# Padding x to 128 rows, splitting the first batch's stores, and retiming two ends of a Fourier and mixture kernel on one Trainium2 core

## The chip, the cores and the metric

The kernel runs on one core of one Trainium2 chip. A core has a matrix engine (PE, whose weight loads are listed as PEld), a vector engine (DVE), a scalar engine (ACT), GpSimd (POOL), and a sync engine (SP) that here issues nearly all DMAs. The metric is device time in microseconds, the median of three runs; one further run was taken with the hardware profiler, and the trace is of that one. Lower is better.

## The reference

For each of 8 batches x is 3136 rows of 256 numbers, float32.

```python
X = np.fft.rfft(x, axis=1)                   # along the 3136 rows
Yr = Xr @ w_r - Xi @ w_i + b_r               # complex product with a 256x256 matrix
Yi = Xr @ w_i + Xi @ w_r + b_i
Y  = soft_threshold(Yr, 0.01) + 1j * soft_threshold(Yi, 0.01)
y  = np.fft.irfft(Y, n=3136, axis=1)
scores = y @ w_gate                          # per row
top = the 128 rows of each batch with the highest scores
out = y;  out[top] += sigmoid(scores[top]) * (relu(y[top] @ w1) @ w2)
```

## The kernel before

3136 is 98 x 32, so the transform is done in two stages. **Stage one** (`s1`) transforms along the 98 rows of a unit, which is one quarter of a pair's columns: a batch has U = 8 units, and two neighbouring units share one load of x (`ld_x`) and one store (`store` inside `s1`). The tile for x has 128 partitions, of which 98 (partitions 15 to 112, two halves of NH = 49) hold data and the rest must be finite; partitions 0 to 14 are set to zero once at the start. A unit can be given to the matmuls as it was loaded (8 matmuls), or first be **folded**: `fold` makes the sum and the difference of the two column halves with two elementwise instructions on DVE or POOL, and then 4 matmuls do. The result goes through a copy on ACT to a tile `at` or `ot` and from there to DRAM (`As`).

**Stage two** (`s2`) reads `As` back transposed: `ld_a(b, g)` with g = 0, 4, 8 loads four groups, each from 16 of the 48 rows of each half, and `s2` transforms along the 32. `spectral` multiplies with the weights (split into two float32r parts each, made by `weights` on DVE), POOL makes the bias tile `kb`, `shrink` does the threshold, and `s2i` goes back along the 32 and writes `Cs` to DRAM. `ld_c` and `s1i` do the inverse along the 98 and store the output. The router (`score`, `select`, `place`) finds the 128 best rows by fixing their threshold digit by digit: each of the eight rounds is a short DVE chain, one small matmul (L254) and again DVE. `fetch` gathers the rows by an indirect DMA on POOL, `ffn` computes the two layers.

The order on every engine is the order in which the code is written; nothing is rescheduled. `units` is a list of T = 100 (batch, group) pairs, and step t of the main loop issues, in this order: stores that were put off (`flush`), loads for later steps, `s2` of unit t + 1, one stage-one unit or inverse unit (`pair`), `spectral` of unit t, folds on POOL, perhaps a second `pair`, and `s2i` of unit t - 1. Before the loop stands the **head**: all of batch 0's stage one, the weights, and 24 matmuls on constants (`warm`). After the loop stands the **tail**: rounds (t counts on from T) in which the last batch's router steps (`turn`), its inverse units and the two layers of the last batches (`work`) take turns; `fill` and `idle` add matmuls on constants. The last batch's gather waits for its rows to be stored, and its two layers come last.

DMAs issued by SP complete through eight semaphores used in turn, so each waits until the eighth DMA before it has landed; all DMAs of one queue share 16 DMA engines.

Of the kernel before, what the change touches and what calls it, by code (L numbers as in the profile page):

```python
# [19 lines left out]
B, S, D = 8, 3136, 256  # L20
N1, N2, NH = 98, 32, 49
# [90 lines left out]
def fourier_moe(ctx: ExitStack, tc: tile.TileContext, x, w_r, w_i, b_r, b_i, wg, w1, w2,  # L112
                t_w, t_wi, t_wq, t_g, t_gi, t_gt, t_gti, t_m, t_dig, outs, cap):
    nc = tc.nc
# [10 lines left out]
    As, Cs, xt, sd, at, ct, av, cv, ot, X, Y, Csc = [{} for _ in range(12)]  # L125
# [4 lines left out]
    def c_tile(shape, dt, name):  # L130
        return const.tile(shape, dt, name=name)
# [6 lines left out]
    xts, cvs = [whole[:, k] for k in range(2)], [c_tile([128, 8, D], F32, "cv" + str(k)) for k in range(2)]  # L138
# [20 lines left out]
    def ld(out, src):  # L159
        nc.sync.dma_start(out=out, in_=src)  # L160
# [188 lines left out]
    def prepare(b, k, idx, xe):  # L349
        n = min(128, cap - 128 * k)  # L350
        px = ps.tile([128, 2, n], F32, name="m", bufs=1)
        for h in range(2):
            nc.tensor.transpose(out=px[:, h, :], in_=xe[:, h * 128:(h + 1) * 128], identity=ident[:n, :n])
        load[0] += 0.25
        xT = pool.tile([128, 2, n], F32, name="xT", bufs=1)
        nc.vector.tensor_copy(xT, px)
        junk = pool.tile([n, D], F32, name="junk", bufs=1)
        sg = pool.tile([n, 1], F32, name="sg")
        nc.vector.tensor_tensor_reduce(out=junk, in0=xe, in1=wgb[:n], scale=1.0, scalar=0.0,
                                       op0=ALU.mult, op1=ALU.add, accum_out=sg)  # L360
        ga = pool.tile([n, 1], F32, name="ga")
        nc.scalar.activation(out=ga, in_=sg, func=AF.Sigmoid)
        return xT, ga

    def pause():
        t = done["t"]
        while done["t"] == t:
            yield

    def hidden(b, k, xT, hs):  # L370
        n = min(128, cap - 128 * k)
        for q in range(FF // 512):
            ph = ps.tile([128, 4, n], F32, name=bank(b, 1 + q % 2), bufs=1)
            for f in range(4):
                if f > 0:
                    yield
                for h in range(2):
                    nc.tensor.matmul(ph[:, f, :], w1s[:, h, (4 * q + f) * 128:(4 * q + f + 1) * 128], xT[:, h, :],  # L378
                                     start=(h == 0), stop=(h == 1))
                load[0] += 0.45  # L380
            hs.append(pool.tile([128, 4, n], F32, name="hh", bufs=2))
            nc.scalar.activation(out=hs[q], in_=ph, func=AF.Relu)
            if done["t"] < T:
                yield from pause()
            else:
                yield

    def combine(b, k, idx, xe, ga, hs):
        n = min(128, cap - 128 * k)
        py = ps.tile([n, D], F32, name=bank(b, 3), bufs=1)  # L390
        for f in range(FF // 128):
            if f > 0:
                yield
            nc.tensor.matmul(py, hs[f // 4][:, f % 4, :], w2s[:, f, :], start=(f == 0), stop=(f == FF // 128 - 1))  # L394
            load[0] += 0.43
        ye = pool.tile([n, D], F32, name="ye", bufs=1)
        nc.vector.scalar_tensor_tensor(out=ye, in0=py, scalar=ga, in1=xe, op0=ALU.mult, op1=ALU.add)
        nc.gpsimd.indirect_dma_start(out=outs[b], out_offset=bass.IndirectOffsetOnAxis(ap=idx, axis=0),
                                     in_=ye, in_offset=None)
        yield  # L400

    def ld_x(b, i):
        if i % 2:
            return
        k = i // 2
        t = (cvs if b < 2 and k > 1 else xts)[k % 2]
        xt[b, k] = t.rearrange("p (h c) d -> p h c d", h=2)
        ld(t[15:113].rearrange("p c d -> p (c d)"), x[b, k])

    def fold(b, i, eng):  # L410
        e = i % 2
        t = xt[b, i // 2][:, :, 2 * e:2 * e + 2, :]
        f = sd[b, i] = pool.tile([128, 2, 2, D], F32, name="sd", bufs=2)
        for k, op in enumerate((ALU.add, ALU.subtract)):
            eng.tensor_tensor(out=f[:113, k], in0=t[:113, 0], in1=t[:113, 1], op=op)  # L415

    def s1(b, i, first=None):
        e = i % 2
        if (e == 0 if first is None else first):
            if b not in As:  # L420
                As[b] = dram.tile([2, NH, N2, D], F32, name="As")
            at[b] = pool.tile([128, 2, 2, 2 * D], F32, name="ot" if b == 0 and i > 3 else "at", bufs=2)
        p = ps.tile([128, 2, 2 * D], F32, name="px" if b == 0 and e else "s", bufs=1)
        if (b, i) in sd:
            f = sd.pop((b, i))
            parts = [[(c, f[:, c])] for c in range(2)]
        else:
            f = [xt[b, i // 2][:, h, 2 * e:2 * e + 2, :] for h in range(2)]
            parts = [[(c, f[0]), (2 * c, f[1])] for c in range(2)]
        for k in range(len(parts[0])):  # L430
            for r in range(2):
                for c in range(2):
                    v, f = parts[c][k]
                    nc.tensor.matmul(p[64 * c:64 * c + 64, r, :], w[64 * r:64 + NH * r, v, :], f[64 * r:64 + NH * r],  # L434
                                     start=(k == 0), stop=(k == len(parts[0]) - 1))
        t = at[b]
        nc.scalar.copy(out=t[:, :, e, :], in_=p)  # L437
        if (e == 0 if first is None else first):
            return
        i = i | 1  # L440

        def store():
            nc.sync.dma_start(out=As[b].rearrange("q m n d -> (q m) n d")[:, 4 * i - 4:4 * i + 4, :], in_=t[15:113])
        stores.append(store)

    def ld_a(b, g):
# [190 lines left out]
    def fill(us):  # L637
        idle(max(0, round((us - load[0]) / 0.216)))
        load[0] = 0.0

    def idle(n):
        if n == 0:
            return
        p = ps.tile([128, 2, 2 * D], F32, name="s", bufs=1)
        for i in range(n):
            nc.tensor.matmul(p[:, 0], wts[0][0][:, 0, :128], wts[0][0].rearrange("p h d -> p (h d)"), start=True, stop=True)

    YB, XB, KB, RB, AB = 2, 2, 1, 1, 2
    G, U = 13, 8
    units = [u for b in range(0, B, 2) for u in [(b, g) for g in range(G)] + [(b + 1, g) for g in range(G - 1)]]  # L650
    units.insert(13, units.pop(12))
    T = len(units)
    LEAD, LAG = 17, 18
    stores, spreads = [], []
    done = {"s2i": -1, "s1i": -1, "t": -1, "c7": 1000, "rep": -1}
    thrs, slots = {}, {}

# [31 lines left out]
    def ffn():  # L689
        for e in range(B * NCHK):  # L690
            while not fetched or done["t"] < age[fetched[0][:2]] or done["t"] < T - 2 and fetched[0][0] > B - 4:
                yield
            item = fetched[0]
            if item[0] == B - 1:
                idle(12)
            xT, ga = prepare(*item)
            if item[0] < B - 1:
                yield from pause()
            else:
                yield  # L700
            hs = []
            yield from hidden(*item[:2], xT, hs)
            yield from combine(*item, ga, hs)
            fetched.pop(0)
# [30 lines left out]
    def flush():  # L735
        for f in stores:
            f()
        del stores[:]
# [4 lines left out]
    for i in range(U):  # L743
        ld_x(0, i)
    warm(8)
    for k, t in enumerate(xts + cvs):
        (nc.gpsimd if k % 2 else nc.vector).memset(t[:15], 0.0)
    consts_a()
    consts_g(0)
    consts_c()  # L750
    for i in range(0, U, 2):
        fold(0, i, nc.vector)
        s1(0, i + 1, True)
        s1(0, i, False)
        flush()
        if i == 4:
            ld_x(1, 0)
    weights()
    warm(24)
    ld_a(0, 0)  # L760
    ld_x(1, 2)
    ld_x(1, 4)
    ld_x(1, 6)
    first = {i - 1: i for i in range(U)}
    fold(1, 0, nc.gpsimd)
    fold(1, 1, nc.gpsimd)
    rest = [(b, i) for b in range(B) for i in range(U)]
    for t in range(-1, T):
# [50 lines left out]
        if 0 <= t - 1 < T:  # L819
            b, g = units[t - 1]  # L820
# [5 lines left out]
    t = T  # L826

    def ready():
        b, i = rest[0]
        return b < B - 1 or t > T + 2  # L830

    def work(us, alone=False):
        turns = 0
# [11 lines left out]
    while threads or ffns:  # L845
        done["t"] = t
        flush()
        load[0] = 0.0
        if t == T:
            work(0.8, True)  # L850
            fill(1.6)
            s2i(*units[T - 1])
            done["s2i"] = B - 1
            flush()
            load[0] = 0.0
            work(0.8, True)
            ld_last(0, 2, True)
            ld_last(2, 1, True)
            ld_last(3, 1, False)
        load[0] = 0.0  # L860
        turn("pe", "da", "db")
        us = 0.4 if t == T else 1.2 if t < T + 11 else 0.6
        work(us, t < T + 2)
        if threads:
            fill(min(us, 1.0))
        t += 1


# [27 lines left out]
```

## Time and profile before

| | us |
|---|---|
| median of 3 runs (lowest, highest) | 698.48 (697.32, 702.02) |
| profiled execution, its own time | 692.63 |
| its span, first to last instruction | 690.4 |

The engines were busy for these shares of the span: PE 94%, PEld 70%, DVE 63%, ACT 53%, POOL 42%. The mean granted PE clock was 0.976 of full. In the chain that ended last PE has 65%, DVE 14%, DMA 7%. A share is a mean over stages with different limits, so the head and the tail are to be read by their own rows.

### The profile page before, as it was taken

The numbers are of one execution on the slowest core, as the hardware profiler recorded it, in microseconds if no ns is written. First come the engines' busy times: TensorE is split into PE (matmuls) and PEld (weight loads), VectorE is DVE, ScalarE is ACT, GpSimd is POOL, SyncE is SP. The second block draws the span as 40 slices with busy tenths as digits, with TensorE's granted clock in tenths as the row PEclk, the third lists the DMA queues.
The fourth block names the chain that finished last, engine by engine and source line by source line (L and its number), as shares of the span: only waits on it lengthen the run. The fifth ranks groups of instructions, "written<-read, shape, count | busy, mean of one in ns | idle before, by whom it ended". The sixth has DMA issues, their size and how long they took to land.

```text
span 690.4 us, 20349 instructions
## 1 busy us (share of the span) xinstructions
PE 650.7 (94%) x8391; PEld 481.8 (70%) x8391; DVE 434.5 (63%) x1384; ACT 364.5 (53%) x672; POOL 287.7 (42%) x243
## 2 busy tenths in 40 slices
PE   7689989999999999999999999999999999998896
PEld 3457767767777777777777777677777777676465
DVE  5326565677687766766677655776587667775531
ACT  3236465566655567655645555655655545554230
POOL 3247555555555555355445443554452222221001
PEclk9889999999999999999999999999999999999779
DMA  8799857798989898979578668879867636978540
GB/s 247 283 261 330 264 168 215 226 303 269 287 258 311 285 304 248 339 222 292 181 213 292 218 226 269 254 251 278 240 207 232 193 117 192 291 230 275 156 149 23
DMA packets 72748, 165.64 MB, mean 240 GB/s; under 512 B 4624, under 2 KB 58354, under 8 KB 60146
## 3 DMA queue, kind: packets, MB, share of 16 engines
q1 hardware_dynamic: 71472, 162.00, 74.7%
q0 software_dynamic: 896, 2.17, 1.1%
q8 instruction: 66, 1.08, 0.7%
q10 hardware_dynamic: 288, 0.18, 0.1%
q14 instruction: 26, 0.21, 0.1%
HBM read 85.23 MB, written 79.17 MB: 238 GB/s over the span
## 4 chain that ended last, share of the span: by engine, by line
PE 65%; DVE 14%; DMA 7%; ACT 5%; issue 5%; POOL 2%; SPq 1%; POOLq 0%; ACTq 0%; DVEq 0%
PE pca L531 10%; PE s L614 6%; DVE junk L543 5%; PE py L233 5%; PE px L470 5%; PE py L234 5%; PE py L235 5%; PE s L434 5%; PE pcb L233 4%; PE m L378 3%; PE m L394 3%; PE pcb L235 2%; PE pcb L234 2%; DVE Xl L483 2%; ACT ct L541 2%
## 5 line engine op out<-in xcount | busy, mean ns | idle before, releaser
L499 POOL TENSOR_TENSOR kb<-ks,bias 128x512 f32<-128x512 f32 x100 | 128.0, 1280 | 308.2 <-ACT ks L497 307.0
L415 POOL TENSOR_TENSOR sd<-xt 113x512 f32<-113x512 f32 x104 | 130.5, 1277 | 31.7 <-DMA xt<-in_x 23.7
L503 DVE TENSOR_TENSOR py<-py,kb 128x512 f32<-128x512 f32 x100 | 70.0, 700 | 80.5 <-POOL kb L499 75.9
L541 ACT COPY ct<-pcb 128x256 f32<-128x256 f32 (+1 forms) x100 | 37.2, 372 | 151.3 <-PE pcb L531 135.0
L531 PE MATMUL pca<-Y,gi_sb 64*64 64x256 f32 x760 | 101.8, 386 | 5.4 <-DVE pca L251 4.8
L483 DVE TENSOR_TENSOR Xl<-px,Xh 128x768 fp32r<-128x768 f32 x100 | 95.7, 957 | 17.6 <-ACT Xh L482 17.4
L531 PE MATMUL pcb<-Y,gi_sb 64*64 64x256 f32 x768 | 103.0, 386 | 0.0
L543 DVE CUSTOM_DVE_ANT_0 junk<-pcb,wgb 128x256 f32<-128x256 f32 (+1 forms) x100 | 42.4, 424 | 88.2 <-ACT ct L541 87.3
L470 PEld LDWEIGHTS px<-g_sb,av 64*64 64x64 f32 x3072 | 78.1, 134 | 16.6 <-issue 2.7
L482 ACT CAST Xh<-px 128x768 fp32r<-128x768 f32 x100 | 81.1, 811 | 14.8 <-PE px L470 13.4
L470 PE MATMUL px<-g_sb,av 64*64 64x96 f32 x3072 | 83.3, 244 | 3.3 <-issue 2.3
L616 ACT COPY ot<-s 128x1024 f32<-128x1024 f32 x58 | 60.1, 1036 | 43.0 <-PE s L614 43.0
L531 PEld LDWEIGHTS pca<-Y,gi_sb 64*64 64x64 f32 x760 | 46.4, 132 | 40.9 <-DVE pca L251 11.5
L508 ACT ACTIVATE r<-py,m2l 128x512 f32<-128x512 f32 x100 | 70.5, 705 | 6.7 <-DVE py L503 6.7
L510 DVE SCALAR_TENSOR_TENSOR Y<-py,r 128x512 f32<-128x512 f32 x100 | 68.5, 685 | 1.6 <-ACT r L508 1.6
L233 PE MATMUL pcb<-wsh,Xh 128*128 128x256 f32 x200 | 65.6, 328 | 1.5 <-DVE Csc L543 1.5
L434 PE MATMUL s<-sd,w 64*64 64x512 f32 x480 | 65.0, 600 | 0.8 <-ACT ot L616 0.8
L614 PE MATMUL s<-cv,wi_sb 64*64 64x512 f32 x464 | 63.0, 612 | 0.0
L437 ACT COPY at<-s 128x1024 f32<-128x1024 f32 x58 | 60.6, 1045 | 3.0 <-PE s L434 2.9
L233 PE MATMUL py<-wnh,Xh 128*128 128x256 f32 x200 | 56.9, 285 | 3.2 <-DVE Y L510 3.0
L234 PE MATMUL pcb<-wsh,Xl 128*128 128x256 f32 x200 | 56.2, 281 | 0.0
L235 PE MATMUL pcb<-wsl,Xh 128*128 128x256 f32 x200 | 56.1, 281 | 0.0
(186 smaller groups left out, 1356.6 us busy)
## 6 DMA issues: line engine op xcount, KB each, us to landing
Cs<-ct SPq DMA_DIRECT2D x48, 512.0 KB
av<-As SPq DMA_DIRECT2D x46, 512.0 KB
As<-at SPq DMA_DIRECT2D x30, 784.0 KB
cv<-Cs SPq DMA_DIRECT2D x30, 784.0 KB
out<-ot SPq DMA_DIRECT2D x30, 784.0 KB
xt<-in_x SPq DMA_DIRECT2D x28, 784.0 KB
cv<-in_x SPq DMA_DIRECT2D x4, 784.0 KB
As<-ot SPq DMA_DIRECT2D x2, 784.0 KB
```

What stands on the lines that cost most here:

```text
L233: nc.tensor.matmul(out, wh, mh, start=start, stop=False)
L234: nc.tensor.matmul(out, wl, mh, start=False, stop=False)
L235: return nc.tensor.matmul(out, wh, ml, start=False, stop=stop).ins
L415: eng.tensor_tensor(out=f[:113, k], in0=t[:113, 0], in1=t[:113, 1], op=op)
L434: nc.tensor.matmul(p[64 * c:64 * c + 64, r, :], w[64 * r:64 + NH * r, v, :], f[64 * r:64 + NH * r], start=(k == 0), stop=(k == len(parts[0 ...
L470: nc.tensor.matmul(o[:, :, N2 * j:N2 * j + N2], a[64 * p:64 * p + 64, j, g % 4, 128 * h + 64 * q:128 * h + 64 * q + 64], g_sb[64 * p:64 * ...
L482: nc.scalar.copy(out=vh, in_=v)
L483: nc.vector.tensor_tensor(out=vl, in0=v, in1=vh.bitcast(F32), op=ALU.subtract)
L499: nc.gpsimd.tensor_tensor(out=kb[:r], in0=ks[:r].broadcast_to([r, 2, D]), in1=bias[:r], op=ALU.add)
L531: nc.tensor.matmul(p[q][64 * a:64 * a + 64], gi_sb[64 * q:64 * q + 64, g, c, 64 * a:64 * a + 64], y[64 * q:64 * q + 64, c, :], start=(c == ...
L543: nc.vector.tensor_tensor_reduce(out=junk[:r], in0=p[k][:r], in1=wgb[:r], scale=1.0, scalar=0.0, op0=ALU.mult, op1=ALU.add, accum_out=Csc[ ...
L614: nc.tensor.matmul(p[64 * c:64 * c + 64, r, :], wi_sb[64 * r:64 + NH * r, b // (B - 1), 15 * c:15 * c + 64], f[64 * r:64 + NH * r, 4 * c + ...
```

## The change

- x is padded on the host with 15 zero rows ahead and 15 behind, and `ld_x` fills all 128 partitions; the four memsets of the first 15 partitions go.
- For batch 0 a pair's store is issued in parts: the first 16 rows of each half at once, the other 32 rows of each half and the two last rows (`others`) later: for the first two pairs after the next pair's or the one behind it, for the last two behind `ld_a(0, 0)`.
- In the head units 4 to 7 are all folded (six units of eight instead of four), on DVE.
- The loads of batch 1's x are all issued behind those stores, the first of them ahead of `ld_a(0, 0)`; batch 1's stage-one units run one step later in the loop (`first`), and so do their folds.
- In the tail the inverse units of the last batch start one round later, a round may take up to 1.3 instead of 1.2 of the planner's units of work up to T + 3, and `idle(12)` is `idle(8)`.

```diff
-        ld(t[15:113].rearrange("p c d -> p (c d)"), x[b, k])
+        ld(t.rearrange("p c d -> p (c d)"), x[b, k])
...
+        v = As[b][:, :, 4 * i - 4:4 * i + 4, :]
+
         def store():
-            nc.sync.dma_start(out=As[b].rearrange("q m n d -> (q m) n d")[:, 4 * i - 4:4 * i + 4, :], in_=t[15:113])
+            if b > 0:
+                ld(v.rearrange("q m n d -> (q m) n d"), t[15:113])
+                return
+            for q in range(2):
+                ld(v[q, :16], t[15 + NH * q:31 + NH * q])
+            later.append(others)
+
+        def others():
+            for q in range(2):
+                ld(v[q, 16:48], t[31 + NH * q:63 + NH * q])
+            ld(v[:, 48], t[63:113:NH])
...
             if item[0] == B - 1:
-                idle(12)
+                idle(8)
...
     warm(8)
-    for k, t in enumerate(xts + cvs):
-        (nc.gpsimd if k % 2 else nc.vector).memset(t[:15], 0.0)
...
     for i in range(0, U, 2):
         fold(0, i, nc.vector)
-        s1(0, i + 1, True)
-        s1(0, i, False)
+        if i > 3:
+            fold(0, i + 1, nc.vector)
+        s1(0, i + (i < 4), True)
+        s1(0, i + (i > 3), False)
         flush()
-        if i == 4:
-            ld_x(1, 0)
+        if i in (2, 4):
+            later.pop(0)()
+    ld_x(1, 0)
     weights()
     warm(24)
     ld_a(0, 0)
-    ld_x(1, 2)
-    ld_x(1, 4)
-    ld_x(1, 6)
-    first = {i - 1: i for i in range(U)}
+    for f in later:
+        f()
+    for i in (2, 4, 6):
+        ld_x(1, i)
+    first = {i: i for i in range(U)}
...
-        return b < B - 1 or t > T + 2
+        return b < B - 1 or t > T + 3
...
-        us = 0.4 if t == T else 1.2 if t < T + 11 else 0.6
+        us = 0.4 if t == T else 1.3 if t < T + 4 else 1.2 if t < T + 11 else 0.6
         work(us, t < T + 2)
         if threads:
-            fill(min(us, 1.0))
+            fill(us if t < T + 5 else min(us, 1.0))
...
     xl = np.asarray(inputs["x"]).reshape(B, 2, NH, 4, 2, 4, D).transpose(0, 3, 4, 2, 1, 5, 6).reshape(B, 4, N1, 8 * D)
+    xl = np.pad(xl, ((0, 0), (0, 0), (15, 15), (0, 0)))
```

How this moves instructions is seen best in the order on each engine. First SP in the head, before: `in_x` is the input, `As` the scratch in DRAM, `av` what `ld_a` fills, and the size is that of the destination.

```order
L160 DMA g_sb<-t_g 128x768
L443 DMA As<-at 98x2048 x2
L443 DMA As<-ot 98x2048
L160 DMA xt<-in_x 98x2048
L443 DMA As<-ot 98x2048
L160 DMA av<-As 128x2x256 x4
L160 DMA xt<-in_x 98x2048
```

And with the change:

```order
L160 DMA As<-at 16x2048 x4
L160 DMA As<-at 32x2048 x2
L160 DMA As<-at 2x2048
L160 DMA As<-ot 16x2048 x2
L160 DMA As<-at 32x2048 x2
L160 DMA As<-at 2x2048
L160 DMA As<-ot 16x2048 x2
L160 DMA xt<-in_x 128x2048
L160 DMA av<-As 128x2x256 x4
L160 DMA As<-ot 32x2048 x2
L160 DMA As<-ot 2x2048
```

Where four stores of 98 rows stood ahead of the reads into `av`, the 16-row parts of all four pairs and the rest of the first two now do; the rest of the last two stands behind them, and the load of x stands right ahead of them instead of ahead of the last store.

Then PE at the end of the head and the start of the loop, before: L434 is `s1` (x8 unfolded, x4 folded), L633 `warm`, L470 `s2`.

```order
L434 MATMUL px<-cv_83,w 64x512 x8
L434 MATMUL s<-sd,w 64x512 x4
L434 MATMUL px<-cv_84,w 64x512 x8
L434 MATMUL s<-sd,w 64x512 x4
L633 MATMUL px<-Xh 128x512 x24
L470 MATMUL px<-g_sb,av 64x3x32 x16
L434 MATMUL s<-sd,w 64x512 x4
L470 MATMUL px<-g_sb,av 64x3x32 x16
```

And with the change, where `warm` is L645 and `s2` L482:

```order
L434 MATMUL s<-sd,w 64x512 x8
L434 MATMUL px<-sd,w 64x512 x4
L434 MATMUL s<-sd,w 64x512 x4
L434 MATMUL px<-sd,w 64x512 x4
L645 MATMUL px<-Xh 128x512 x24
L482 MATMUL px<-g_sb,av 64x3x32 x32
L434 MATMUL s<-sd,w 64x512 x4
```

Sixteen matmuls of two units became eight, and the first two `s2` stand next to each other, with no stage-one unit between them.

Last PE in the tail, before, from the second digit's matmul (L254) on: L614 is an inverse unit, L394 the second layer, L328 the end of `place` for the batch before the last.

```order
L254 MATMUL pcb<-digits,n 128x15
L328 MATMUL pca<-row,hot 128x34
L328 MATMUL pca<-neg,hot 128x34
L328 MATMUL pca<-row,hot 128x34
L328 MATMUL pca<-neg,hot 128x34
L614 MATMUL s<-xt,wi_sb 64x512 x4
L394 MATMUL py<-w2s,hh 128x256
L254 MATMUL pcb<-digits,n 128x15
L614 MATMUL px<-xt,wi_sb 64x512 x4
L394 MATMUL py<-w2s,hh 128x256
L254 MATMUL pcb<-digits,n 128x15
```

And with the change, where an inverse unit is L626:

```order
L254 MATMUL pcb<-digits,n 128x15
L328 MATMUL pca<-row,hot 128x34
L328 MATMUL pca<-neg,hot 128x34
L328 MATMUL pca<-row,hot 128x34
L328 MATMUL pca<-neg,hot 128x34
L394 MATMUL py<-w2s,hh 128x256 x4
L254 MATMUL pcb<-digits,n 128x15
L626 MATMUL s<-xt,wi_sb 64x512 x4
L626 MATMUL px<-xt,wi_sb 64x512 x4
L254 MATMUL pcb<-digits,n 128x15
```

Four second-layer matmuls now stand ahead of the third digit, the first inverse unit behind it, and then two inverse units stand between two digits where one of them and a second-layer matmul stood.

## Rows read from the trace of the kernel before

**Rows 1.** Sums by stretch: us, length, busy by engine (instructions), granted clock, DMA share, GB/s.
```profile
34.60:60.00 25.40, 22.91 (x303) 16.20 (x304) 10.46 (x20) 12.79 (x21) 14.15 (x13) 0.87 0.97 286
160.00:300.00 140.00, 137.75 (x1941) 102.87 (x1941) 100.13 (x329) 86.83 (x161) 69.85 (x57) 1.00 0.91 292
647.30:664.40 17.10, 17.10 (x68) 7.15 (x67) 8.36 (x43) 5.52 (x7) 1.01 (x1) 0.50 0.41 129
62.50:64.50 2.00, 2.00 (x16) 1.52 (x13) 1.93 (x4) 2.00 (x4) 1.00 (x1) 1.00 1.06 430
```

**Rows 2.** Instructions by time on DVE, head: start, length, what, [idle before <- what ended it].
```profile
6.93 1.29 DVE L415 TENSOR_TENSOR sd<-xt 113x512 f32<-113x512 f32 x2 [1.24 <-DMA xt<-in_x]
...
13.53 1.29 DVE L415 TENSOR_TENSOR sd<-cv 113x512 f32<-113x512 f32 x2 [1.87 <-DMA cv<-in_x]
16.49 1.29 DVE L415 TENSOR_TENSOR sd<-cv 113x512 f32<-113x512 f32 x2 [1.67 <-PE px L434]
...
22.82 0.48 DVE L628 MEMSET Y<- 128x512 f32 x1
```

**Rows 3.** Instructions by time on SP, head.
```profile
21.50 0.31 SPq L443 DMA_DIRECT2D As<-ot  x1
31.79 1.92 SPq L160 DMA_DIRECT2D av<-As  x4
```

**Rows 4.** Instructions by time on PE, end of the head and first steps.
```profile
24.01 8.27 PE L633 MATMUL px<-Xh 128*128 128x512 f32 x24 [3.66 <-ACT Xh L630]
34.61 1.24 PE L470 MATMUL px<-g_sb,av 64*64 64x96 f32 x32 [2.33 <-issue]
35.67 1.30 PE L434 MATMUL s<-sd,w 64*64 64x512 f32 x8
37.82 1.56 PE L470 MATMUL px<-g_sb,av 64*64 64x96 f32 x32 [0.85 <-DVE Xl L483]
...
44.27 0.89 PE L470 MATMUL px<-g_sb,av 64*64 64x96 f32 x32
...
48.87 0.35 PE L233 MATMUL py<-wnh,Xh 128*128 128x256 f32 x1 [1.51 <-DVE Y L510]
...
51.39 0.84 PE L470 MATMUL px<-g_sb,av 64*64 64x96 f32 x32
...
56.29 0.84 PE L470 MATMUL px<-g_sb,av 64*64 64x96 f32 x32
```

**Rows 5.** Instructions by time on POOL, first steps.
```profile
45.28 1.27 POOL L499 TENSOR_TENSOR kb<-ks,bias 128x512 f32<-128x512 f32 x1
```

**Rows 6.** Instructions by time on PE, tail.
```profile
645.39 1.09 PE L614 MATMUL s<-xt,wi_sb 64*64 64x512 f32 x8 [1.42 <-DMA xt<-Cs]
...
650.40 1.99 PE L614 MATMUL s<-xt,wi_sb 64*64 64x512 f32 x8
...
665.36 0.23 PE L294 MATMUL pca<-tm,mask 98*64 98x98 bf16 x1
...
671.09 3.70 PE L394 MATMUL py<-w2s,hh 128*128 128x256 f32 x16
674.44 3.10 PE L646 MATMUL s<-wsh 128*128 128x512 f32 x12
677.38 0.38 PE L353 MATMUL m<-ident,xe 128*128 128x128 f32 x2
```

**Rows 7.** Instructions by time on DVE, tail.
```profile
645.30 0.16 DVE L251 TENSOR_TENSOR pcb<-digits,pcb 128x1 uint32<-128x1 uint32 x1
647.28 0.17 DVE L261 TENSOR_SCALAR ok<-pcb 128x15 f32<-128x15 f32 x1 [1.81 <-PE pcb L254]
648.62 0.16 DVE L251 TENSOR_TENSOR pcb<-digits,pcb 128x1 uint32<-128x1 uint32 x1
```

**Rows 8.** The gathers (L342): the last by time, and the line's issue to landing.
```profile
673.08 0.97 POOL L342 DMA_INDIRECT xe<-out,idx  x1 [11.12 <-DMA out<-ot]
DMA to landing us min/median/max: 2.7/6.3/8.3
```

More of the change, by code (lines that the diff above doesn't have):

```diff
@@ L653, in fourier_moe @@
     LEAD, LAG = 17, 18
-    stores, spreads = [], []
+    stores, spreads, later = [], [], []
     done = {"s2i": -1, "s1i": -1, "t": -1, "c7": 1000, "rep": -1}
```

## The prediction

> **What bounds the kernel now.** I read the sums by stretch first, for the granted clock and PE's idle time, then PE, DVE and SP in order of time at both ends. In the long middle PE is the bound: in 140 us it is busy for 137.75 at full clock, beside a DMA share of 0.91 [rows 1]. Nothing the change touches can help there, so its worth lies in the head and the tail.
>
> In the head three waits follow each other. The loads of x arrive 3.3 us apart (folds that wait for them start at 6.93 and 13.53, two loads later), and the fourth fold waits for PE, not for its load [rows 2]. The last store is issued at 21.50, yet SP can issue the reads of `av` only at 31.79, when all of it has landed [rows 3]. So PE, though it fills 24.01 to 32.28 with constant matmuls, waits 2.33 us for its first `s2` at 34.61 [rows 4]. Then the clock is low: 0.87 over 25.4 us is 6.6 us at half, 1.2 instead of 2.4 GHz [rows 1]. The third `s2` is 6.45 us behind the second and the fourth 7.12 behind that, where the next needs 4.90 [rows 4]. Part of the 7.12 is a wait of 1.51 for `Y` [rows 4]: POOL made the first `kb` only at 45.28, with no idle time before it, since a fold stood ahead in its queue [rows 5].
>
> In the tail the third digit's matmul stands behind the first inverse unit, which waits 1.42 us for its data; the digit was ready at 645.30 + 0.16 [rows 6, 7]. PE, which stood still until 645.39, has half the clock from 647.3 to 664.4 although it is then busy for all 17.1 us [rows 1, 6]. An inverse unit takes 1.99 us there, against 1.09 before [rows 6].
>
> **The head, step by step.** *Loads of x.* They grow from 803 to 1049 KB. No row shows a 128-row load of x. At the old rate (803 KB in 3.3 us, 243 GB/s) one takes 4.3 us; at the 430 GB/s of the stretch in which 128-row loads of tables dominate, 2.4 us [rows 1]. I take 2.5 to 3.0, nearer the second, as it is a 128-row load too; up to 3.3 the result is the same, because folds and copies then bound the head. The Trainium skill ("DMA: Bandwidth & Descriptors", the section on why a DMA increments its semaphore by 16) speaks against this: a transfer runs on the largest number of engines up to 16 that divides its rows, so 98 rows go over 14 and 128 over 16, and each engine gets 8 rows for 7. Estimated by that page a load takes 3.3 x 8/7 = 3.8 us, and the sum below would lose 1.8 us. No row here shows the engines of a load apart. The memsets that go are worth nothing: the first fold waited for its load, not for DVE [rows 2].
>
> *Stage one.* Two more units folded are 2 x 1.29 us on DVE [rows 2] and save PE about 1 us each. A fold needs the tile of the second fold before it, and a unit the bank of the unit two before it, so a pair still takes about the 2.96 us between the last two folds [rows 2]. The last copy ends near 21.3 (before: the store at 21.50) [rows 3]. Last fold's end: 19.1 in place of 17.78. `weights` stands behind it on DVE and takes 5.5 us to 23.30 [rows 2], so `warm` starts at 24.01 + 1.4 = 25.4. Its 24 matmuls took 8.27 us [rows 4], at full clock 24 x 3.10/12 = 6.2 [rows 6]; I take 7.6 and a first `s2` at 33.0 (31.6 to 33.7).
>
> *Stores and reads.* The reads of `av` now wait for 16-row parts alone. The last part is issued near 21.7 and lands about 23.5. Then a load of x (2.4 us) is ahead of `av` on the DMA engines, and 0.5 MB of `av` serves the first `s2`: ready near 28.5, bounds 27 and 31. Either is covered by `warm` until 33.0; without that cover it would be worth another 2 to 5 us. The 20 stores in place of 4 each wait on SP for the eighth DMA before them, but 14 are issued while PE and DVE finish the head and the other 6 stand behind `av`.
>
> *First steps.* `s2` number two no longer has a stage-one unit before it: it waits the 2.15 us from 35.67 to 37.82 in which both copies of the first are made [rows 4], so it starts at 33.0 + 1.06 + 2.15 = 36.2, not 37.82: **-1.6**. From there to the third, 6.45 us at half clock become about 4.0 (4.90 without the 0.9 of `s2i`): **-2.4**. From the third to the fourth, 4.90 for 7.12, as `kb` now stands ahead of the fold on POOL: **-2.2**. The stage-one unit that moved out returns at step 7, whose data is there: **+1.0** (1.30 with some half clock in row 35.67). The wait of 2.15 us may bring the clock down again; half the chance of 1.7 us is **+0.8**. Head: **-4.4**, between -7 and +2.4 (loads at 4.3 us each).
>
> **The tail.** Four second-layer matmuls, 8 instructions of 3.70/16 us [rows 6], fill PE from the end of `place` (645.39 - 1.42 = 643.97) to 645.8; the third digit follows at once instead of behind the first inverse unit and one such matmul, and the data of that unit, for which PE waited until 645.39, has then landed. PE no longer waits 1.42 us there, and I expect the clock to stay up. A round is then two inverse units at 1.05 and a digit at 0.3, 2.4 us; the DVE part of 1.50 (647.28 to 648.78) [rows 7] fits beside them. Three rounds bring the sixth digit to 653.1, the next two (one unit each, and the transposes) the last to 657.3, and the mask's matmul comes at 658.6, not 665.36 [rows 6]: **-6.8**. From there to the last transposes it was 12.02 us. Fewer first-layer matmuls stand between `place`'s steps, and `idle(8)` saves 4 x 0.26; I count 6.9 us to the gather and its 2.7 us to landing [rows 8], 9.6: **-2.4**. The gather waited for the last output store [rows 8]; with the last unit near 656 that lands near 661 and is no bound. Tail: **-9.2**, between -10.5 and -1.5. The rest of the end, from 677.38, is the same.
>
> **Sum.** The profiled execution took 692.63 us: 692.63 - 4.4 - 9.2 = 679.0. The median of the timed runs lies 5.85 above it, which I keep: **685**.
>
> **Rivals.** *The clock falls in the tail all the same.* Two inverse units at 1.99 and a digit are then 4.4 us a round, and PE has the same work at half clock. For it: the fall at 647.3 came with PE busy again for 2 us, and while busy it stayed low for 17 us [rows 1]. Against: the idle time before it goes. Tail -2, so 698.5 - 4.4 - 2 = 692. Chance 0.18.
>
> *Loads at eight rows per engine take 3.8 us.* The fourth x lands 2 us later and the whole head chain through `weights` and `warm` shifts 1.8: 687. The page above states this; the 430 GB/s speak against it. Chance 0.10.
>
> *The head's time is given back.* If the queue (share 0.97 from 34.6 to 60 [rows 1]) holds `av` for the fifth group or the x of the first steps late, PE waits there instead: head 0, total 689. Chance 0.10.
>
> *Slower.* The queue becomes the bound of the middle. If the rate of an x load and not its rows is fixed, each takes 1.0 us longer, on engines busy 0.91 in the stretch [rows 1]; PE hardly waits for DMA there now. It decides when that share reaches 1.0. The head is then 2.4 us worse, and if half of 24 x 1.0 us shows on PE, even with the tail's gain it is 698.5 + 2.4 + 12 - 9.2 = 704, and 713 without. Chance 0.05.
>
> That the change is void in the tail (the order on PE the same) is excluded by the order shown ahead; in the head the reads could still wait for whole stores, but then `s2` comes near 34 and only about 1 us is lost.
>
> **How the numbers follow.** The forecast, with 0.57, spans 678 to 691: the median's 5.85 may shrink or stay, head and tail move within their bounds. With the rivals the range is **677 to 694**. About 1%, 7 us, is what a measurement of this kernel tells from no change, so faster begins at 691.5. Faster: most of the forecast (0.54), a third of the first rival, most of the next two: 0.75. Slower over 1%: 0.05. Within: 0.20.
>
> **What would show it.** Right: folds of x 2.5 to 3 us apart; `av` issued near 23.5; `warm` running straight into `s2` near 33; no wait for `Y` near 41; fourth `s2` near 45; granted clock 1.00 from 640 to 680, rounds of 2.4 us, the last gather near 665. Wrong: a clock of 0.50 anywhere after 640, or PE waiting for a DMA between 45 and 75. If the middle's DMA share rises past 0.95 with PE waiting for it, the slower rival holds.

## The result and the profile after

| | before | changed |
|---|---|---|
| median of 4 runs each on one chip, us | 700.25 | 678.38 |
| lowest, highest | 697.32, 702.46 | 677.42, 681.79 |
| profiled execution, its own time | 692.63 | 677.42 |
| its span, and mean granted clock | 690.4, 0.976 | 675.5, 0.995 |

The ratio is 0.9699, with a 95% interval of 0.9644 to 0.9754: faster, as forecast, and 6.6 us below the forecast of 685, inside its range. The ratios here and below leave a kernel's slow runs out, so where before has runs near 686 a ratio can stand closer to 1 than the medians do.

Between the two profiles 14.9 us of span went. Three marks on PE divide them: the first digit's matmul of the last batch (640.07, now 634.00: 6.07 won in the head), the mask's matmul (665.36, now 652.45: 6.84 more) and the last transposes (677.38, now 662.49: 1.98 more). From there to the end nothing changed.

First the sums by stretch of the changed kernel (columns as in [rows 1]), for the first steps, the middle, and the tail from the first inverse unit to the mask and on to the last transposes.

```profile
31.60:60.00 28.40, 25.32 (x369) 18.58 (x370) 13.50 (x27) 14.80 (x26) 19.10 (x16) 0.94 0.85 306
160.00:300.00 140.00, 137.38 (x1939) 102.85 (x1936) 100.18 (x328) 86.55 (x161) 72.31 (x58) 1.00 0.87 298
...
640.46:652.45 11.99, 11.78 (x92) 5.36 (x92) 7.84 (x41) 7.91 (x9) 1.01 (x1) 1.00 0.86 281
652.45:662.49 10.04, 8.92 (x54) 7.58 (x53) 2.81 (x16) 1.20 (x2) 1.97 (x2) 1.00 0.29 98
```

The middle is what it was (PE 137.38 of 140 us); its DMA share fell from 0.91 to 0.87 in spite of the padded loads. The tail has its full clock throughout, where [rows 1] has 0.50. Next DVE in the head, by time (columns as in [rows 2]).

```profile
6.40 1.29 DVE L415 TENSOR_TENSOR sd<-xt 113x512 f32<-113x512 f32 x2 [4.99 <-DMA xt<-in_x]
9.18 1.29 DVE L415 TENSOR_TENSOR sd<-xt 113x512 f32<-113x512 f32 x2 [1.48 <-DMA xt<-in_x]
11.71 1.29 DVE L415 TENSOR_TENSOR sd<-cv 113x512 f32<-113x512 f32 x2 [1.24 <-DMA cv<-in_x]
13.31 1.29 DVE L415 TENSOR_TENSOR sd<-cv 113x512 f32<-113x512 f32 x2 [0.31 <-PE s L434]
15.59 2.50 DVE L415 TENSOR_TENSOR sd<-cv 113x512 f32<-113x512 f32 x4 [0.98 <-PE s L434]
...
23.13 0.48 DVE L640 MEMSET Y<- 128x512 f32 x1
```

The folds that wait for x start at 6.40, 9.18 and 11.71, 2.65 us apart on average in place of 3.3; the folds behind them wait for PE. SP in the same stretch, by time:

```profile
21.75 1.61 SPq L160 DMA_DIRECT2D As<-ot  x2
23.47 0.36 SPq L160 DMA_DIRECT2D xt<-in_x  x1
25.40 1.92 SPq L160 DMA_DIRECT2D av<-As  x4
```

From the issue of the last two parts that `av` waits for to the issue of `av` it is now 3.65 us, where the last whole store took 10.29 [rows 3]. PE from the constant matmuls on, by time:

```profile
24.32 7.24 PE L645 MATMUL px<-Xh 128*128 128x512 f32 x24 [5.09 <-ACT Xh L642]
31.62 0.89 PE L482 MATMUL px<-g_sb,av 64*64 64x96 f32 x32
34.48 1.56 PE L482 MATMUL px<-g_sb,av 64*64 64x96 f32 x32 [1.97 <-DVE Xl L495]
35.81 1.93 PE L434 MATMUL s<-sd,w 64*64 64x512 f32 x8
...
39.99 0.89 PE L482 MATMUL px<-g_sb,av 64*64 64x96 f32 x32
...
45.14 0.43 PE L543 MATMUL pca<-Y,gi_sb 64*64 64x256 f32 x2 [0.72 <-DMA gi_sb<-t_gi]
...
46.06 0.84 PE L482 MATMUL px<-g_sb,av 64*64 64x96 f32 x32
```

`warm` runs straight into the first `s2`, 2.99 us sooner than in [rows 4]; the fourth `s2` is 5.33 sooner. Behind the wait of 1.97 us the clock is low for a short stretch (1.56 for an `s2` that takes 0.89). The wait of 1.51 for `Y` is gone, since POOL makes the first `kb` at 39.17 ahead of a fold that starts at 40.42 ([rows 5]: 45.28). A new, smaller one of 0.72 has come, for the table `gi_sb` of `s2i`. PE in the tail, by time:

```profile
639.55 0.30 PE L254 MATMUL pcb<-digits,n 128*128 128x15 f32 x2
640.46 1.09 PE L626 MATMUL s<-xt,wi_sb 64*64 64x512 f32 x8 [0.61 <-DMA xt<-Cs]
641.34 1.07 PE L626 MATMUL px<-xt,wi_sb 64*64 64x512 f32 x8
642.34 0.39 PE L254 MATMUL pcb<-digits,n 128*128 128x15 f32 x2
...
644.60 0.39 PE L254 MATMUL pcb<-digits,n 128*128 128x15 f32 x2
...
652.45 0.23 PE L294 MATMUL pca<-tm,mask 98*64 98x98 bf16 x1
...
662.49 0.41 PE L353 MATMUL m<-ident,xe 128*128 128x128 f32 x2 [1.12 <-DMA xe<-out,idx]
```

The third digit stands ahead of the first inverse unit, whose wait is 0.61 in place of 1.42 [rows 6]; inverse units stay at 1.09 us, and a round of two of them and a digit takes 2.2 to 2.3 us, where a round with a single unit took 3.3 (units of 1.99 us [rows 6]). The last gather on POOL, issued at 673.08 in [rows 8], is now issued 13.48 us sooner:

```profile
659.60 0.97 POOL L342 DMA_INDIRECT xe<-out,idx  x1 [18.08 <-PE py L394]
```

### The profile page after: what moved, and what is told of

Read it like the earlier page. It is cut to its first block, busy times and chain, and to the rows that moved or that the text cites. A ratio compares the mean times of both kernels' runs of the same rounds, so it can differ in the third digit from the quotient of the medians.

```text
span 675.5 us, 20324 instructions
## 1 busy us (share of the span) xinstructions
PE 636.5 (94%) x8371; PEld 475.3 (70%) x8371; DVE 433.4 (64%) x1386; ACT 363.5 (54%) x672; POOL 284.3 (42%) x241
## 4 chain that ended last, share of the span: by engine, by line
PE 61%; DVE 14%; DMA 7%; issue 6%; ACT 5%; POOL 4%; SPq 1%; POOLq 0%; ACTq 0%; DVEq 0%
PE pca L543 10%; PE s L626 5%; DVE junk L555 5%; PE py L233 5%; PE px L482 5%; PE py L234 4%; PE py L235 4%; PE s L434 4%; PE pcb L233 4%; PE m L378 3%; PE m L394 3%; DVE Xl L495 2%; PE pcb L235 2%; PE pcb L234 2%; POOL kb L511 2%
## 5 line engine op out<-in xcount | busy, mean ns | idle before, releaser
L482 PEld LDWEIGHTS px<-g_sb,av 64*64 64x64 f32 x3072 | 77.9, 134 | 14.2 <-DVE Xl L495 2.2
L482 PE MATMUL px<-g_sb,av 64*64 64x96 f32 x3072 | 83.0, 244 | 2.0 <-DVE Xl L495 2.0
L434 PE MATMUL s<-sd,w 64*64 64x512 f32 x480 | 64.4, 599 | 2.3 <-ACT at L437 1.2
L626 PE MATMUL s<-cv,wi_sb 64*64 64x512 f32 x464 | 61.4, 598 | 0.0
```

Source lines behind the costliest of these rows:

```text
L482: nc.tensor.matmul(o[:, :, N2 * j:N2 * j + N2], a[64 * p:64 * p + 64, j, g % 4, 128 * h + 64 * q:128 * h + 64 * q + 64], g_sb[64 * p:64 * ...
L626: nc.tensor.matmul(p[64 * c:64 * c + 64, r, :], wi_sb[64 * r:64 + NH * r, b // (B - 1), 15 * c:15 * c + 64], f[64 * r:64 + NH * r, 4 * c + ...
```

## The experiments

The experiments ran on different chips, and before's median lay between 697.16 and 700.25 beside them. A difference of 1 to 2 us between two variants of the changed kernel is therefore not told by medians alone; the profiles say which wait it is.

**The tail alone.** Before, with these lines:

```diff
-                idle(12)
+                idle(8)
...
-        return b < B - 1 or t > T + 2
+        return b < B - 1 or t > T + 3
...
-        us = 0.4 if t == T else 1.2 if t < T + 11 else 0.6
+        us = 0.4 if t == T else 1.3 if t < T + 4 else 1.2 if t < T + 11 else 0.6
...
-            fill(min(us, 1.0))
+            fill(us if t < T + 5 else min(us, 1.0))
```

> The kernel before with the tail's edits alone (inverse units one round later, rounds of 1.3, 8 instead of 12 constant matmuls); head, loads and stores as before. Theory: PE no longer waits for the first inverse unit's data, so the granted clock stays at 1.00 from 640 to 665; a round takes 2.2 to 2.4 us instead of 3.3, the mask's matmul comes 6 to 7 us earlier counted from the end of the loop, the last gather another 2 us: the profiled span falls by 8 to 10 us, ratio about 0.985. Rival: the gain of the change lies in the head and in the fewer constant matmuls, and the tail's order is worth nothing by itself: about 1 to 2 us, ratio 0.997 to 0.999, half clock from 647 on as before.

Measured: 685.02 us against 698.95, ratio 0.9836 (0.9772 to 0.9900); span 681.0, 9.4 below before's. The first digit stands at 639.92, where it was; from it to the mask 17.91 us in place of 25.29, to the last transposes 10.08 in place of 12.02, and no half clock in either stretch. So it is as the theory had it, and the rival's 1 to 2 us are out. By the medians it is more, 13.9 us; why is taken up with the prediction below.

**The head alone.** The changed kernel with those lines as they were before.

> The changed kernel with the tail's edits undone: padded loads, folds, divided stores and the later second batch stay. Theory: the head's 5 to 6 us stay (first digit near 634, as in the changed kernel), the tail takes what it took before (first digit to the last transposes 37 us, with half clock and rounds of 3.3 us): span about 684.5, ratio about 0.992. Rival: the shift by 6 us alone lets the data of the first inverse unit be there, or the clock stay up; then the tail is short too, span about 676.

Measured: 692.68 us (689.41 to 696.31) against 698.95; ratio 1.0016 (0.9961 to 1.0070); span 690.2. The tail came out as the theory said: 26.44 us from the first digit to the mask, at half clock. PE there, by time:

```profile
645.25 1.11 PE L626 MATMUL s<-xt,wi_sb 64*64 64x512 f32 x8 [2.58 <-DMA xt<-Cs]
...
647.30 0.45 PE L254 MATMUL pcb<-digits,n 128*128 128x15 f32 x2
647.67 1.99 PE L626 MATMUL px<-xt,wi_sb 64*64 64x512 f32 x8
```

Its head did not. The same code reached the first digit at 638.76, not near 634: the wait for `gi_sb` was 2.19 us here, and half clock followed it. PE at that place:

```profile
47.59 0.43 PE L543 MATMUL pca<-Y,gi_sb 64*64 64x256 f32 x2 [2.19 <-DMA gi_sb<-t_gi]
...
48.51 1.18 PE L482 MATMUL px<-g_sb,av 64*64 64x96 f32 x32
49.44 1.95 PE L434 MATMUL s<-sd,w 64*64 64x512 f32 x8
```

By this profile the head is worth 1.3 us, by the changed kernel's 6.1, by the medians 6.3; the interval of the ratio has 1 in it. That the head's edits alone make the kernel faster is therefore not shown beyond the noise.

**Constant matmuls in the wait.** Before, with one addition:

```diff
+                if rest[0] == (B - 1, 0):
+                    idle(7)
```

> The kernel before with 7 constant matmuls (about 1.5 us) put on PE directly ahead of the last batch's first inverse unit, where PE waited 1.42 us for data; the order of all other work is the old one. Theory: the granted clock falls at 647 because PE stood still there, so with the matmuls it stays at 1.00, inverse units take 1.09 instead of 1.99 us, rounds about 2.2 us, and the mask's matmul comes 5 to 8 us earlier: ratio 0.988 to 0.993. Rival: the order of digit and inverse unit is what counts, not the clock: the matmuls fill time that was empty, the clock falls as before, span the same or up to 1.5 us longer.

Measured: 688.00 us against 698.95, ratio 0.9883 (0.9814 to 0.9951). PE, by time:

```profile
647.66 1.09 PE L614 MATMUL s<-xt,wi_sb 64*64 64x512 f32 x8 [0.70 <-DMA xt<-Cs]
...
649.22 0.29 PE L254 MATMUL pcb<-digits,n 128*128 128x15 f32 x2
649.44 1.09 PE L614 MATMUL px<-xt,wi_sb 64*64 64x512 f32 x8
...
651.11 0.39 PE L254 MATMUL pcb<-digits,n 128*128 128x15 f32 x2
```

The order is before's; inverse units take 1.09 us, a round 2.0, and the mask comes 19.55 us after the first digit, 5.74 less than before. So the clock, not the order, is most of what was won ahead of the mask.

**Before, once more**, unchanged:

> The kernel before once more, unchanged, for a second profile of it: its runs lie between 685 and 701 us, while the one profiled took 692.63 and the changed kernel's lie within 677 to 682. Theory: the runs differ by how long the granted clock stays at half, in the head and from 647 on; this profile shows either a longer half clock in one of the two places or, in a run near 687, none in the tail. Rival: they differ by waits for DMAs in the middle of the kernel, with the clock the same.

Measured: 689.65 us, span 687.4. This profile is of another kind than the first: the head is 4.45 us later (first `s2` at 39.06), and the tail keeps its clock. PE, by time:

```profile
644.62 0.30 PE L254 MATMUL pcb<-digits,n 128*128 128x15 f32 x2
...
649.15 1.09 PE L614 MATMUL s<-xt,wi_sb 64*64 64x512 f32 x8 [0.62 <-DMA xt<-Cs]
...
650.70 0.29 PE L254 MATMUL pcb<-digits,n 128*128 128x15 f32 x2
...
662.38 0.23 PE L294 MATMUL pca<-tm,mask 98*64 98x98 bf16 x1
```

The unchanged code needs 17.76 us here from the first digit to the mask: 7.53 less than in its other profile; what differs on PE ahead of the fall is the wait for the first inverse unit, 0.62 for 1.42. The profiles so far line up on that: after waits of 1.42 and 2.58 the clock fell, after 0.61, 0.62 and 0.70 it did not. The length of the wait alone is no rule, though. The third try below waited 1.22 there and kept its clock, and in the head of before a longer wait than the tail's, the 1.51 for `Y` [rows 4], was followed by full clock (columns as in [rows 1]):

```profile
48.87:56.00 7.13, 7.13 (x98) 5.65 (x102) 3.95 (x9) 4.13 (x8) 5.08 (x5) 1.00 0.94 348
```

What else decides stays open. And the head varies: SP issued the last store at 23.52 and `av` at 36.28.

```profile
23.52 0.31 SPq L443 DMA_DIRECT2D As<-ot  x1
36.28 1.92 SPq L160 DMA_DIRECT2D av<-As  x4
```

The theory held for the tail; in the head of this profile it was the store, issued 2.02 us later and 12.76 us ahead of the next instead of 10.29 [rows 3], and not the clock.

**x in 98 rows.** The changed kernel, with this load, before's four memsets, and no padding on the host:

```diff
-        ld(t.rearrange("p c d -> p (c d)"), x[b, k])
+        ld(t[15:113].rearrange("p c d -> p (c d)"), x[b, k])
```

> The changed kernel with x loaded in 98 rows again (partitions 15 to 112, zeros written once by memsets), all else as changed. Theory: the loads of x arrive 3.3 us apart instead of 2.65, so the fourth comes about 2 us later, but PE's and DVE's own work of the head fills most of that; the head loses 1 to 2 us and the middle nothing: ratio to the kernel before about 0.972. Rival: the faster padded loads carry the head's gain: 5 us of it are lost, ratio about 0.978. A third: with 24% fewer bytes per load the middle gets shorter instead, ratio below 0.968.

Measured: 681.42 us against 698.95, ratio 0.9781 (0.9716 to 0.9846); span 679.4. DVE, by time:

```profile
6.97 1.29 DVE L415 TENSOR_TENSOR sd<-xt 113x512 f32<-113x512 f32 x2 [1.29 <-DMA xt<-in_x]
10.52 1.29 DVE L415 TENSOR_TENSOR sd<-xt 113x512 f32<-113x512 f32 x2 [2.25 <-DMA xt<-in_x]
13.94 2.50 DVE L415 TENSOR_TENSOR sd<-cv 113x512 f32<-113x512 f32 x4 [2.12 <-DMA cv<-in_x]
17.54 2.50 DVE L415 TENSOR_TENSOR sd<-cv 113x512 f32<-113x512 f32 x4 [1.10 <-DMA cv<-in_x]
```

The loads come 3.5 us apart, the first `s2` stands at 34.72 (31.62 with padding) and the fourth at 50.08 (46.06), with a wait of 1.9 for `gi_sb`. My theory of 1 to 2 us fell: the rival is nearer, for the span is 3.9 us longer. The third fell as well.

**Whole stores.** The changed kernel, with all of a pair stored at once:

```diff
-            if b > 0:
+            if True:
                 ld(v.rearrange("q m n d -> (q m) n d"), t[15:113])
                 return
...
-            later.pop(0)()
+            pass
```

> The changed kernel with batch 0's stores whole again, all four issued before the first reads. Theory: SP can issue av only when all of the last store has landed, some 2 to 4 us later than 25.40; the constant matmuls end at 31.5, so the first s2 comes 2 to 4 us later with PE idle ahead of it: 2 to 4 us slower than the changed kernel, median 680 to 683. Rival: the bytes ahead of av on the DMA engines and not its issue decide, as the other parts then come right behind av anyway; then at most 1 us.

Measured: 679.90 us against 698.66, ratio 0.9729 (0.9682 to 0.9775); span 677.9. `av` is issued at 29.01, the first `s2` comes at 33.59 after a wait of 1.06, the fourth at 48.41. It is the theory's mechanism at its lower end: 2.4 us of span, 1.5 of the median.

**The second x at its old step.**

```diff
-    first = {i: i for i in range(U)}
+    first = {i - 1: i for i in range(U)}
```

> The changed kernel with batch 1's stage-one units at their old step of the loop, one earlier (so is the third fold on POOL). Theory: one unit of 1.0 us stands between the first two s2's where PE has 1.97 us to wait anyway, but it waits there for the fold of the late x, and the fold ahead of kb on POOL brings back a wait of about 1 us for Y: 1 to 2 us slower. Rival: the unit fills the wait and keeps the clock up, so it is as fast or 1 us faster.

Measured: 679.55 us against 698.66, ratio 0.9729 (0.9682 to 0.9776); span 677.1. The third `s2` comes at 39.24, 0.75 sooner, and no half clock follows; then a wait of 1.52 for `Y`, with waits of 1.03 for the folds, brings the fourth to 48.22, 2.16 later. The theory holds in the profile, the median's 1.2 us is inside the spread.

**Four tries to better the head.** The first moves `gi_sb`:

```diff
     consts_g(0)
+    consts_gi(0)
     consts_c()
...
-        if t in (-1, 1, 4, 9):
+        if t in (1, 4, 9):
```

> The changed kernel with the first table of s2i (gi_sb) and wgb loaded in the head behind the first part of g_sb, where the DMA engines stand nearly idle from 15 to 17 us, instead of behind batch 1's x. Theory: the wait for gi_sb (0.72 us in the changed kernel's profile, 2.19 in that of the head alone, 1.9 with 98 rows) is what is late next in the head and differs between runs; without it the fourth s2 comes near 45.0 instead of 46.06 and no half clock follows behind it: 1 to 2 us less, median near 677. Rival: the bytes only change places on a full queue; the stores or the reads of av come later by 1 us and the time is the same.

Measured: 679.52 us against 698.66, ratio 0.9720 (0.9675 to 0.9764). The wait for `gi_sb` is gone, but SP issues the last 16-row stores at 25.19, not 21.75, and `av` at 27.88; PE waits 3.31 for it, and the fourth `s2` comes at 49.92. The rival had it, and more than its 1 us: between 15 and 17 us the DMA engines were not nearly idle, as I had it, but had shares of 0.42 and 0.35 in the changed kernel, and 0.94 in the next microsecond.

The second has also x early, and other constant matmuls:

```diff
+        if i == 2:
+            ld_x(1, 0)
         if i in (2, 4):
             later.pop(0)()
-    ld_x(1, 0)
     weights()
-    warm(24)
+    warm(14)
...
             s2(*units[t + 1])
+        if t == -1:
+            idle(8)
```

> The changed kernel with three more edits in the head: gi_sb as in the run before; batch 1's first x issued during stage one instead of between the stores and av; 14 constant matmuls instead of 24 ahead of the first s2, and 8 between the first and the second. Theory: av was served behind 1 MB of x, so it now lands 2 us earlier, the first s2 comes near 29.5 instead of 31.6; the constant matmuls in the 1.97 us wait hold the granted clock at 1.00 behind 34 (worth 1.0 to 1.7 us): all in all 4 to 5 us, median near 674. Rival: the last stores are served behind that x instead, so av is no earlier; then PE waits ahead of its first s2 with 14 matmuls done, the clock falls longer, and the time is the same as the changed kernel's or 2 us more.

Measured: 680.34 us against 698.66, ratio 0.9732 (0.9688 to 0.9777). `av` was issued at 29.68, PE waited 3.37 for it: the rival. The clock fell behind that wait, so the 8 matmuls took 3.33 us and delayed the second `s2`.

The third leaves only the 16-row stores ahead of `av`:

```diff
-        if i in (2, 4):
-            later.pop(0)()
-    ld_x(1, 0)
-    weights()
-    warm(24)
+    warm(22)
+    weights()
     ld_a(0, 0)
+    ld_x(1, 0)
+    later.pop(0)()
+    consts_gi(0)
     for f in later:
         f()
...
-        if t in (-1, 1, 4, 9):
+        if t in (1, 4, 9):
```

> The changed kernel with only the eight 16-row stores of batch 0 issued ahead of av: the other parts, batch 1's first x and gi_sb come behind av (x first, then one pair's parts, then gi_sb, then the rest), and the constant matmuls (22 for 24) stand ahead of the weights on DVE and ACT, so that PE can begin them near 21 instead of 24.3. Theory, after the two early-load runs: what holds av is SP's row of waits, each store for the eighth DMA ahead of it, and the last store's landing, not the bytes; with 6 stores fewer ahead, the last 16-row store is issued near 20.5 instead of 21.75 with no queue before it, av near 22.5 instead of 25.40, landed near 25.5 with no x ahead, and the first s2 comes near 26 instead of 31.6: 4 to 6 us less than the changed kernel, median 673 to 675. Rival: the loads that are moved behind av are then late themselves (x for the fold at the first stage-one unit, gi_sb, x of the next pairs), and PE waits there: the fourth s2 within 1 us of the changed kernel's 46.06, the same time.

Measured: 683.78 us against 697.22, ratio 0.9867 (0.9747 to 0.9988). The first `s2` came at 27.41, 4.21 sooner; then PE waited 4.14 for the fold of x, and the fourth came at 48.83, the fifth 5.34 later than in the changed kernel. It is the rival's wait, at more than the rival's price. Its first inverse unit in the tail, on PE by time, and the next but one:

```profile
647.03 1.09 PE L626 MATMUL s<-xt,wi_sb 64*64 64x512 f32 x8 [1.22 <-DMA xt<-Cs]
...
649.25 1.09 PE L626 MATMUL s<-xt,wi_sb 64*64 64x512 f32 x8
```

The fourth adds to the third x early, and one unit between the first `s2`s (lines against the third try):

```diff
+        if i == 2:
+            ld_x(1, 0)
-    warm(22)
+    warm(24)
     weights()
     ld_a(0, 0)
-    ld_x(1, 0)
     later.pop(0)()
     consts_gi(0)
...
-    first = {i: i for i in range(U)}
+    first = {i - (i == 0): i for i in range(U)}
```

> The run with few stores ahead of av (constant matmuls ahead of the weights, other parts and gi_sb behind av), with two edits: batch 1's first x is issued during stage one, ahead of the last two pairs' stores, and batch 1's first unit alone stands between the first two s2's, the other seven as in the changed kernel. Theory: in the run before, PE lost its head start by the wait of 4.14 us for the fold of that late x and by the 13.65 us of half clock behind it; with x early the fold is done before 26, the unit fills the 1.97 us wait and holds the clock, and av, with no x ahead of it, lands near 27: first s2 near 28, fourth near 43 instead of 46.06: 2 to 3 us less than the changed kernel, median near 676. Rival: the 1 MB of x ahead of the last stores delays them as it did in the kernel before (28 us or later for the issue of av): then 0 to 2 us slower than the changed kernel.

Measured: 681.41 us against 697.16, ratio 0.9840 (0.9707 to 0.9973). PE, by time:

```profile
27.89 1.18 PE L482 MATMUL px<-g_sb,av 64*64 64x96 f32 x32 [0.48 <-DMA av<-As]
...
42.88 0.84 PE L482 MATMUL px<-g_sb,av 64*64 64x96 f32 x32
...
46.44 3.20 PE L434 MATMUL s<-sd,w 64*64 64x512 f32 x8 [2.73 <-POOL sd L415]
...
54.66 0.84 PE L482 MATMUL px<-g_sb,av 64*64 64x96 f32 x32
```

The two times expected up to the fourth `s2` came (28 and 43, measured 27.89 and 42.88, 3.18 sooner than in the changed kernel), though the clock was not held: PE waited 2.21 us ahead of the third, which took 1.56. One step on it was lost: the next pair's x, now behind all the other stores, was late for its fold, and the fifth `s2` is 3.7 us later. What failed was the theory's step from there to the end.

With that unit alone moved,

```diff
-    first = {i: i for i in range(U)}
+    first = {i - (i == 0): i for i in range(U)}
```

> The changed kernel with batch 1's first stage-one unit alone moved one step earlier, between the first two s2's; the other seven units and all folds stay. Theory: in the run with all eight units a step earlier the third s2 came 0.75 us sooner and no half clock followed 34 us, but a fold ahead of kb on POOL cost 1.5 us; with one unit moved the first stays and the second is not there: 1 to 2 us less than the changed kernel, median 676.5 to 677.5. Rival: the fold of x is late (0.9 us of wait in that run), and gi_sb, 0.72 us late already, eats what is won: the same time.

Measured: 680.75 us against 697.16, ratio 0.9829 (0.9696 to 0.9962). The third `s2` stands at 39.50 and the wait for `gi_sb` at 2.67: the rival. No version has a lower median than the changed kernel's 678.38, and those within 2 us of it are not told apart from it.

**What they have in common.** I took from each profile the sum of the stretch up to the fifth `s2`; bytes are its rate times its length.

| | fifth `s2` | GB/s to there | MB | DMA share |
|---|---|---|---|---|
| changed kernel | 50.95 | 334 | 17.0 | 0.91 |
| one unit moved | 54.01 | 319 | 17.2 | 0.93 |
| fourth try | 54.66 | 313 | 17.1 | 0.91 |
| head alone (same head as changed) | 54.97 | 314 | 17.3 | 0.92 |
| third try | 56.29 | 301 | 16.9 | 0.90 |
| 98 rows | 54.97 | 277 | 15.2 | 0.94 |

The four variants left out lie among these (53.12 to 54.81 us, shares of 0.88 to 0.92). Up to there the DMA engines are busy for nine tenths of the time and move much the same bytes whatever the order, and in each of the tries some load was late (`av` twice, x twice, `gi_sb` once). That the bytes set the end of the head is not shown: the same 17 MB took 50.95 to 56.29 us at nearly one share, 15.2 MB took as long as 17.3, and no run took bytes away at the same rate.

## Why the prediction was right, and where its sizes were not

*The tail* was right in cause and size: to the mask -6.8 forecast, -6.84 measured; to the transposes -2.4 and -1.98. No row shows the data of the first inverse unit "landed" by then; the wait shrank to 0.61, and that was enough. One reading was too narrow: I took half clock there as a property of before. It is one of two outcomes, so the tail's edits are worth 9.4 us against one profile of before, and about 2 where the wait is short anyway, since 17.91 and 17.76 us to the mask are the same.

*The head* gave 6.07, not 4.4, inside its bounds, and partly by luck: the second `s2` came 3.34 us sooner in place of 1.6, and the smaller gains behind it happen to add up to 2.73, as near as can be to the 2.8 forecast, from other terms. Loads of x at 2.5 to 3.0 us: 2.65. Last fold's end 19.1: 18.09; first `s2` 33.0: 31.62. Second to third `s2` fell by 0.94, not 2.4 (6.45 to 5.51), since the clock fell once more, to which I had given half a chance (+0.8). Third to fourth fell by 1.05, not 2.2, because `gi_sb` was late; that wait was not in my sum, and in three of the variants it was 1.9 to 2.7. With its 0.72 us, up to 45.14, it meets one sign of being wrong to the letter: PE waiting for a DMA between 45 and 75. The returning unit cost nothing: with it the step takes 4.91 us (70.97 to 75.88), without it 4.89. The last 0.74 us came between the fourth `s2` and the first digit, in no single place.

*The issue of `av`* was at 25.40, not 23.5, but its cover, `warm`, held to the end, as supposed.

*The 5.85 us* between the profile and the median were the failing term: I carried them over, and only 0.96 came. The profiles sum to 692.63 - 6.07 - 6.84 - 1.98 = 677.74, beside 677.42. Most of the rest seems to lie in the tail and not in the stores. The run of the tail alone has before's head and stores, and by the medians it is 13.9 us below before, 4.5 more than the 9.4 between the profiles; the constant matmuls in the wait gave 10.95 by the medians and 4.4 between the profiles. (The intervals of both ratios reach some 4.5 us to either side, so these sizes are rough.) The clocks agree: the four runs of each of the two have 0.988 to 0.994, before's runs beside them 0.970 to 0.989. By an estimate from span and mean clock, a run of before with span 698.6 and clock 0.97 has 2 x 0.03 x 698.6 = 41.9 us of half clock and the profiled one 33.1; 8.8 us more at half clock cost 4.4. Where in such a run they lie stays open, as no profile of one is there. Before's second profile adds that the head can come 4.45 us later behind a late store; that the divided stores end this is not shown, as whole stores in the changed kernel cost only 2.4 us of span.

*The rivals.* The clock did not fall in the tail. Loads at 3.8 us did not come. By the rule of the Trainium skill ("DMA: Bandwidth & Descriptors", the section named in the prediction) 128 rows go over 16 engines and 98 over 14. The estimate from that count alone made 128 rows the slower ones; the folds, 2.65 against 3.5 us apart, decide against the estimate. No trace here shows the engines of a load apart, so the count itself is not tested. The head was in part given back, by `gi_sb`; more than that in the profile of the head alone. The slower rival is out: the share in the middle fell to 0.87.

## What to carry to other kernels

Where PE stands still ahead of a long dense stretch, fill or shorten that wait first, and read the granted clock behind it: a stall of 1.4 us cost 7.5 in the tail here, one of 0.6 or 1.2 in the same place nothing, and one of 1.5 in the head no clock either. Before a forecast, compare one profile's time with the spread of the runs; where they differ, part of a change's worth is that it ends a bad outcome which the profile may not show. And where the DMA engines are busy for nine tenths of a stretch, work out which load becomes late before moving another one forward.

## Not expected of the hardware

A load of x with 128 rows came faster than one with 98, though it has 31% more bytes (1049 for 803 KB in 2.65 and 3.3 to 3.5 us). The number of rows and the first partition (0 for 15) changed together, and no run tells the two apart. The same shows over the whole head: a DMA share of 0.94 moved 277 GB/s with 98 rows, 0.91 moved 334 with 128. And PE's clock, once down in the tail, stayed at half for 17 us in which PE was busy throughout [rows 1], while the same instructions with full clock from the start kept it.
